# Square roots on ScalarE, an earlier warm-up and block transposes in a planned attention-plus-SwiGLU kernel

## The chip, the cores and the metric

The kernel runs on one core of a Trainium2 chip. A core has TensorE (PE, matrix multiplication into PSUM), VectorE (DVE), ScalarE (ACT), GpSimd (POOL) and SyncE (SP, which here only starts DMAs). Each takes its instructions in a fixed order from a queue of its own and waits on semaphores for the others. The metric is the device time of one execution in microseconds (us). The profile shows one execution; its span is the time from the first to the last instruction that it records.

## What is computed

All arrays are bfloat16, with 2048 rows of 512 values, 32 heads of 16 values, and a gated layer 1792 wide.

```python
xn  = layernorm(A_x)                          # no scale, no shift, eps 1e-5
q, k, v = split(xn @ wqkv)                    # 32 heads of 16
p   = softmax(q @ k.T / 4)                    # per head, 2048 x 2048
att = (p @ v).reshape(2048, 512) @ wo
ffn = (silu(xn @ w1) * (xn @ w3)) @ w2
out = A_x + att + ffn
```

## The kernel before

The heads are taken in 8 groups of four, and the queries in 4 chunks of 512. One chunk of one group is cut into *units* of 256 queries (128, 128, 256 in the first; 128 each in the last four); there are 73 units, numbered from 0. Each unit goes through these stages:

- **Pass 1** (line 1059 and line 1099). Two matmuls, one for each of two heads, write scores of 128 queries by 512 keys into two PSUM banks, and one DVE reduction takes the maximum of these 1024 columns. There are two such pairs of banks, so the next pair's matmuls run while DVE reduces. Three *splits* (lines 1088, 1168) save DVE a reduction each: ScalarE writes the Relu of a difference of two score blocks twice, and one custom DVE operation of 1024 columns takes the place of two reductions.
- **The maximum into the queries.** When a unit's reductions are done, its negated maximum (line 1235 on DVE, or six small POOL operations) becomes two more rows of the query matrix. For the first two and last four units this goes by a matmul and a copy into QT (line 821 on ScalarE; line 817 on DVE for the last unit); for the others by three DMAs.
- **Pass 2** (lines 1321, 1334, 1364). Scores again, keys by queries, with the maximum already subtracted, and ScalarE's exponential from PSUM into the buffer PT, 512 columns at a time or two banks in one instruction.
- **PV** (line 572). The exponentials against V, with a column of ones that yields the softmax denominator as row 16 of each head's 32 rows. Normally ScalarE copies the result out, and three DMAs and two POOL operations (lines 1445 to 1469) invert the denominators and multiply. For the last three units ("fast", `NFPV = 3`) DVE does it: a shuffle that copies row 16 over its head's rows, a reciprocal of 128 by 128, a multiplication (lines 1409 to 1412).
- **Column work** on TensorE between these: K, Q and V projections, the gated layer (`G`, `U`), the output (`OUT`; `OUTA` and `OUTB` for the last chunk).

**The head** is what happens before pass 1 can flow. The input lies in 16 tiles of 128 rows. For each pair of tiles the mean and variance come from DVE (lines 605, 608; tiles 0 to 7) or from two ScalarE passes (lines 595, 599; tiles 8 to 15). POOL then computes the reciprocal root by a power (lines 619, 622), and DVE (tiles 0 to 5, line 635) or POOL (tiles 6 to 15, after lines 626 and 628; line 645) normalizes. TensorE transposes a tile (line 670), and ScalarE copies it into `xnT` (line 677). Four tiles give one 512-key block of K for the first group: matmuls of line 568 and the ScalarE copy of line 701, which this text calls `KT0` to `KT3`. Pass 1 of units 0 to 2 (32 reductions) begins with the 8 that need `KT0` alone, goes on with 8 on `KT1`, and so on. While TensorE has no data it multiplies a tile of ones (line 1675); that is the warming.

**What sets the order.** A planner in the same file builds the kernel: it holds a model of each engine (when it is free, how long an operation takes, when its result is seen) and picks, over and over, the operation that can start first. `pick_pe` chooses between pass 1, pass 2, column work and filling; `pick_act`, `pick_dve`, `pick_pool` and `pick_sp` do the same for their engines. The resulting lists are what the engines run, in that order. The constants at the head of `_build` are thresholds of this planner: `_COLD` is the time up to which it counts a matmul as twice as long, `TOL` how far a piece of column work may run past the time at which a score matmul is due, `FFN_LO` and `FFN_HI` between which reductions the gated layer is spread, `SPLIT_STEP` every how many units a split stands, `PV_LEFT` how many exponentials may be missing when PV starts.

Of the kernel before, what the change touches and what calls it, by code (L numbers as in the profile page):

```python
# [13 lines left out]
_COLD = 5.9  # L14
# [239 lines left out]
def _build(nc, A_x, A_wqkv, A_wo, B_w1, B_w3, B_w2, out):  # L254
# [7 lines left out]
    NQC = S // 512  # L262
# [17 lines left out]
    TAIL_MATE = 0.3  # L280
# [3 lines left out]
    HI_LEAD = 0.0  # L284
    LAZY_MAX = 3.0
# [5 lines left out]
    A_LEAD = 0.69  # L291
# [17 lines left out]
    NFPV = 3  # L309
    NXR = 2  # L310
    FFN_LO = -60
    FFN_HEAD = 12
    FILL_P1 = 1
    FFN_HI = 800
# [5 lines left out]
    TAIL_LOW = 0  # L320
    TAIL_HIGH = 3
# [5 lines left out]
    URG_WAIT = 0.12  # L327
    FILL_SLIP = 0.03
# [3 lines left out]
    SPLIT_STEP = 6  # L332
# [21 lines left out]
    with ctx:  # L354
# [10 lines left out]
        mhalf = sb("mhalf", [128, NT], FP32)  # L365
        mone = sb("mone", [128, 8], FP32)
# [95 lines left out]

        P.op("pool", lambda e: e.memset(ones_t[:, :], 1.0), writes=[("ones_t",)], occ=0.2)
# [15 lines left out]
        P.op("dve", lambda e: e.memset(bank(7), 0.0), writes=[("ps", 7)], occ=0.5)  # L479
        P.op("pe", lambda e: e.matmul(bank(4)[:, 0:1], maskrow, onesrow[:, 0:1], start=True, stop=True),  # L480
# [7 lines left out]
        NORM = "dddppppp"  # L488
        STATS = "ddddaaaa"
        landed = [DMA_FIRST]  # L490
# [40 lines left out]
        def pad(dst, src, g):  # L531
# [5 lines left out]
                for g in range(NG - NPADQ, NG)}  # L537
        miscq.append(_Item(lambda e: e.activation(dk, sk, ACTF.Identity), [("wk",)], [("wk0",)], 0.3,
                           cb=lambda op: done.add("wk0")))
        miscq.append(_Item(lambda e: e.activation(dq, sq, ACTF.Identity), [("wq",)], [("wq0",)], 0.3,  # L540
                           cb=lambda op: done.add("wq0")))
# [44 lines left out]
        def ln_chunk(gi):  # L586
# [6 lines left out]
            if on_act:  # L593
                for t in tl:
                    act_stats.append(_Item(lambda e, t=t: e.activation(
                        a32[:, :], x_sb[:, t, :], ACTF.Identity, scale=1.0 / D, accum_out=mv[:, t, 0:1]),
                        [("PT", t)], [("a32",), ("mv", t)], 0.57, 0.7))
                for t in tl:
                    act_stats.append(_Item(lambda e, t=t: e.activation(
                        a32[:, :], x_sb[:, t, :], ACTF.Square, scale=-1.0, bias=mv[:, t, 0:1],  # L600
                        accum_out=mv[:, t, 1:2]),
                        [("PT", t), ("mv", t)], [("a32",), ("mv", t)], 0.66, 0.8, cb=lambda op: mv_done(op)))
            else:
                for t in tl:
                    dveq.append(_Item(lambda e, t=t: e.bn_stats(stats[:, t, :], x_sb[:, t, :]),
                                      [("PT", t)], [("st", t)], 0.6, 0.7, cb=lambda op, t=t: done.add(("st", t))))
                for t in tl:
                    dveq.append(_Item(lambda e, t=t: e.bn_aggr(mv[:, t, :], stats[:, t, :]), [("st", t)], [("mv", t)],
                                      0.075, 0.2, pred=lambda t=t: ("st", t) in done, cb=lambda op: mv_done(op),
                                      name="hi" if t == t1 - 1 else ""))  # L610
# [5 lines left out]

            def coef(op):
                q = poolq["ln"]
                q.append(_Item(lambda e: e.tensor_scalar(lnt[:, sl_], mv[:, sl_, 1], 1.0 / D if on_act else 1.0, EPS,
                                                         ALU.mult, ALU.add),  # L620
                               MVK, [("lnt", gi)], 0.25, 0.35))
                q.append(_Item(lambda e: e.tensor_tensor(lnr[:, sl_], lnt[:, sl_], mhalf[:, sl_], ALU.pow),
                               [("lnt", gi), ("mhalf",)], [("lnr", gi)], 0.4 + 0.16 * (t1 - t0),
                               0.5 + 0.16 * (t1 - t0), cb=norm if NORM[gi] == "d" else None))
                if NORM[gi] != "d":
                    q.append(_Item(lambda e: e.tensor_tensor(lnt[:, sl_], mv[:, sl_, 0], lnr[:, sl_], ALU.mult),
                                   [("lnr", gi)] + MVK, [("lnt", gi)], 0.25, 0.35))
                    q.append(_Item(lambda e: e.tensor_scalar(lnb[:, sl_], lnt[:, sl_], -1.0, 0.0, ALU.mult, ALU.add),
                                   [("lnt", gi)], [("lnb", gi)], 0.25, 0.35, cb=norm))

            def norm(op):
                for t in tl:
# [6 lines left out]
                    elif NORM[gi] == "a":  # L639
                        miscq.append(_Item(lambda e, t=t, xs=xs: e.activation(  # L640
                            xn_sb[:, xs, :], x_sb[:, t, :], ACTF.Identity, scale=lnr[:, t:t + 1], bias=lnb[:, t:t + 1]),
                            [("PT", t), ("lnr", gi), ("lnb", gi)], [("osb", xs)], 0.71, 0.85,
                            cb=lambda op, t=t: tr_ready(t), pred=lambda t=t: t < 4 or ("tr", t - 4) in done))
                    else:
                        poolq["nx"].append(_Item(lambda e, t=t, xs=xs: e.tensor_scalar(
                            xn_sb[:, xs, :], x_sb[:, t, :], lnr[:, t:t + 1], lnb[:, t:t + 1], ALU.mult, ALU.add),
                            [("PT", t), ("lnr", gi), ("lnb", gi)], [("osb", xs)], 0.7, 0.8,
# [142 lines left out]
        def tile_QT(q0, nq, name):  # L790
            def evac(bk):
                def cb(op):
# [3 lines left out]
                    else:  # L796
                        miscq.extend(act_stats[PRE_STATS:])
                return [_Item(lambda e: e.activation(QT[:, 0, q0:q0 + nq], bank(bk)[:, 0:nq], ACTF.Identity),
                              [("ps", bk)], qh_keys(0, q0, nq), _c_act(nq), cb=cb)]
# [573 lines left out]
        def tile_PV(u):  # L1373
# [26 lines left out]
            def evac(bk):  # L1400
                if fast:
# [7 lines left out]
                    return [_Item(lambda e: e.stream_shuffle(rp, bank(bk)[:, 0:nq], [16] * 32), [("ps", bk)],  # L1409
                                  RK, 0.21, 0.33),  # L1410
                            _Item(lambda e: e.reciprocal(rp, rp), RK, RK, 0.985, 1.13),
# [131 lines left out]
        def assign():  # L1543
# [26 lines left out]
            if p1_left[0] > 1 and p1_n[0] > 0 and not head_tiles:  # L1570
                for bk in (6, 5, 4):
                    if bk not in bank_tenant and p2_n[0] == 0:
                        if crit and ok(crit[0]):
                            give(crit.pop(0), bk)
# [6 lines left out]
        def rank(t):  # L1581
            return 0 if t.name.startswith("AQ") else 1.5 if t.name.startswith("V") else 2 if t.name.startswith("OUTB") else 1
# [84 lines left out]
        def warm_cand():  # L1667
            for bk in (5, 4):
# [3 lines left out]
                st = P.pe_start("col", None, P.ready("pe", [("ones_t",)], writes))  # L1672

# [39 lines left out]
        def pick_pe():  # L1713
# [3 lines left out]
            f = fill_cand() if ("QT", 0) in done else warm_cand()  # L1717
            def fits(x, limit):
# [66 lines left out]
        def pick_act():  # L1785
# [13 lines left out]
            for k, it in enumerate(miscq[:14]):  # L1799
                if okp(it):  # L1800
                    s = cand("act", it)
                    r = {"first": 0, "second": 1}.get(it.name, 2)
                    if m is None or s < m[0] - 1e-6 or (s < m[0] + 1e-6 and r < m[2]):
                        m = (s, k, r)
# [28 lines left out]
        def pick_dve():  # L1833
            b = None
            for q, depth in ((dveq, 8), (redq, 1)):
                for k, it in enumerate(q[:depth]):
                    if okp(it):
                        s = cand("dve", it)
                        if it.name == "hi":
                            s = max(s - HI_LEAD, 0.0)  # L1840
                        if b is None or s < b[0] - 1e-6:
                            b = (s, q, k)
            return None if b is None else (b[0], lambda: emit_item("dve", b[1], b[2]))

        def pick_pool():
            b = None
            for k in ("z", "ln", "nx", "split", "nrm", "ffn", "pad"):
                q = poolq[k]
                if q and okp(q[0]):
                    s = cand("pool", q[0])  # L1850
                    if b is None or s < b[0] - 1e-6:
                        b = (s, q)
            return None if b is None else (b[0], lambda: emit_item("pool", b[1], 0))
# [10 lines left out]
        for gi in range(len(LN_GROUPS)):  # L1864
            ln_chunk(gi)
        miscq.extend(act_stats[:PRE_STATS])
# [87 lines left out]
```

## Time and profile before

| what | value |
|---|---|
| median of 3 runs (lowest to highest) | 1194.18 us (1193.86 to 1194.46) |
| the profiled execution, own time | 1194.38 us |
| its span | 1192.6 us |
| busy: PE, DVE, ACT, POOL | 96%, 98%, 98%, 38% |
| granted TensorE clock | 0.998 of full speed |
| first and last pass-1 reduction start or end | 13.65 us, 1170.6 us |
| first and last exponential | 46.0 us, 1186.8 us |

A row of a timeline gives the start in us, the duration in us, the engine, the line, the operation, output and input, and how many were merged; a bracket tells how long the engine was idle before and for whom. Durations overlap a little, because an engine begins an instruction before the last one has been written out: the distance between two starts (the *pitch*) is what an instruction costs its queue. A row of the groups gives the busy time, the mean duration in ns, and the idle time before.

### The profile page before, as it was taken

The page shows a single profiled execution, that of the slowest core. Times are in us where ns is not written, and L with a number is a line of the kernel's source. Part 1 is how long each engine was busy: PE and PEld are TensorE (multiplying, and loading weights), DVE is VectorE, ACT ScalarE, POOL GpSimd, SP SyncE. Part 2 cuts the span into 40 slices and gives each one's busy share as a digit, 9 for nine tenths or more (in the row PEclk, how much of TensorE's full clock was granted, in tenths as well). Part 3 has the DMA queues.
Part 4 walks back from the last instruction along what each step waited for, and adds up shares of the span by engine and source line. Part 5 has one row for each costly group of instructions (what it writes and reads, how often), then busy time and mean ns, then how long its engine had stood idle before and what let it go on. Part 6 is the DMA issues. An engine that isn't in the chain of part 4 may idle for free.

```text
span 1192.6 us, 33530 instructions
## 1 busy us (share of the span) xinstructions
PE 1149.6 (96%) x13972; PEld 477.7 (40%) x13972; DVE 1173.6 (98%) x1076; ACT 1168.0 (98%) x2227; POOL 456.8 (38%) x912
## 2 busy tenths in 40 slices
PE   9999999999999999999999999999999999999997
PEld 5443333333334333333333434343333333345554
DVE  8999999999999999999999999999999999999995
ACT  7899999999999999999999999999999999999998
POOL 4453743433432246344422236734222125343320
PEclk9999999999999999999999999999999999999999
DMA  6523322111111021111100122211000111001000
GB/s 183 127 60 80 71 65 79 39 33 42 36 25 38 24 68 45 37 37 29 35 20 24 36 54 50 47 41 37 23 20 16 36 28 44 22 19 21 18 18 24
DMA packets 131188, 52.16 MB, mean 44 GB/s; under 512 B 100068, under 2 KB 131036, under 8 KB 131036
## 3 DMA queue, kind: packets, MB, share of 16 engines
q1 hardware_dynamic: 131036, 50.01, 16.8%
q8 instruction: 110, 1.80, 0.6%
q14 instruction: 42, 0.34, 0.1%
HBM read 38.73 MB, written 6.74 MB: 38 GB/s over the span
## 4 chain that ended last, share of the span: by engine, by line
ACT 43%; PE 41%; DVE 13%; issue 2%; DMA 1%; POOL 0%; ACTq 0%; POOLq 0%
ACT PT L1334 29%; PE ps L568 15%; DVE part L1099 13%; PE ps L1321 12%; ACT PT L1364 7%; PE ps L572 7%; PE ps L1059 6%; ACT zg L867 1%; ACT th L861 1%; ACT ub L871 1%; ACT U L1424 1%; ACT kq L756 1%; PE ps L1675 1%; ACT xnT L677 0%; ACT Vaug L771 0%
## 5 line engine op out<-in xcount | busy, mean ns | idle before, releaser
L1099 DVE TENSOR_REDUCE part<-ps 128x2 f32<-128x1024 f32 x1018 | 1153.0, 1212 | 1.9 <-PE ps L1059 1.7
L1334 ACT ACTIVATE PT<-ps 128x512 bf16<-128x512 f32 x1668 | 882.7, 626 | 4.5 <-PE ps L1321 1.5
L1321 PE MATMUL ps<-QT,KT 32*128 32x256 bf16 (+1 forms) x4672 | 543.4, 259 | 4.5 <-ACT PT L1364 3.7
L1059 PE MATMUL ps<-KT,QT 32*128 32x512 bf16 x2042 | 423.7, 383 | 2.4 <-DVE part L1099 2.3
L1321 PEld LDWEIGHTS ps<-QT,KT 32*128 32x128 bf16 x4672 | 206.4, 92 | 213.8 <-issue 110.9
L1449 POOL TENSOR_TENSOR Rc<-Lc,mone 128x8 f32<-128x8 f32 (+1 forms) x70 | 106.0, 1515 | 293.7 <-DMA Lc<-U 293.6
L1364 ACT ACTIVATE PT<-ps 128x1024 bf16<-128x1024 f32 x190 | 200.5, 1071 | 0.1
L568 PE MATMUL ps<-xnT,ident 128*128 128x512 bf16 (+3 forms) x642 | 176.3, 341 | 17.8 <-DVE part L1099 6.7
L572 PE MATMUL ps<-PT,Vaug 128*17 128x256 bf16 (+1 forms) x4672 | 177.3, 261 | 5.3 <-ACT PT L1364 2.2
L568 PE MATMUL ps<-xnT,w 128*128 128x512 bf16 (+3 forms) x637 | 153.1, 321 | 4.6 <-ACT ub L871 1.3
L1059 PEld LDWEIGHTS ps<-KT,QT 32*128 32x128 bf16 x2042 | 107.2, 91 | 122.9 <-DVE part L1099 57.8
L572 PEld LDWEIGHTS ps<-PT,Vaug 128*17 128x17 bf16 x4672 | 82.2, 89 | 91.5 <-issue 69.7
L568 PEld LDWEIGHTS ps<-xnT,ident 128*128 128x128 bf16 x642 | 47.0, 97 | 100.0 <-ACT PT L1334 44.6
L568 PEld LDWEIGHTS ps<-xnT,w 128*128 128x128 bf16 x637 | 44.9, 97 | 85.7 <-issue 53.0
L568 PE MATMUL ps<-w,hT 128*128 128x512 bf16 (+3 forms) x330 | 75.0, 315 | 0.0
L848 POOL TENSOR_TENSOR a<-zg,ub 128x512 f32<-128x512 bf16 x56 | 64.6, 1154 | 21.4 <-ACT ub L871 21.3
L850 POOL TENSOR_TENSOR hT<-a,t 128x512 bf16<-128x512 f32 x56 | 71.0, 1268 | 2.4
L1206 POOL TENSOR_TENSOR mx<-part 128x16 f32<-128x16 f32 (+1 forms) x67 | 14.2, 211 | 138.3 <-DVE part L1099 137.8
L1469 POOL TENSOR_TENSOR wk_on<-U,R 128x256 bf16<-128x256 f32 (+1 forms) x37 | 23.4, 632 | 88.3 <-DMA R<-rd 88.2
L1469 POOL TENSOR_TENSOR on_b<-U,R 128x256 bf16<-128x256 f32 (+1 forms) x33 | 23.4, 710 | 73.6 <-DMA R<-rd 73.6
L846 POOL TENSOR_SCALAR t<-th 128x512 f32<-128x512 bf16 x56 | 34.8, 622 | 43.0 <-ACT th L861 41.2
L861 ACT ACTIVATE th<-zg 128x512 bf16<-128x512 bf16 x56 | 37.6, 671 | 0.0
(106 smaller groups left out, 563.7 us busy)
## 6 DMA issues: line engine op xcount, KB each, us to landing
w<-in_B_w_dram SPq DMA_DIRECT2D x112, 128.0 KB
R<-rd SPq DMA_DIRECT2D x55, 128.0 KB
QT<-qd SPq DMA_DIRECT2D x31, 128.0 KB
KT<-kd SPq DMA_DIRECT2D x28, 128.0 KB
PT<-in_A_x_dram SPq DMA_DIRECT2D x4, 512.0 KB
xr<-in_A_x_dram SPq DMA_DIRECT2D x16, 128.0 KB
out_dram<-osb SPq DMA_DIRECT2D x16, 128.0 KB
qd<-kq SPq DMA_DIRECT2D x15, 128.0 KB
```

The costliest lines, as they stand in the source:

```text
L568: return e.matmul(bank(bk)[:, c0 + a:c0 + b], make_lhsT(0, 128), rhs_ap(0)[:, a:b], start=start, stop=stop, **kw)
L572: ins = e.matmul(bank(bk)[32 * i:32 * i + m, c0 + a:c0 + b], make_lhsT(i), rhs if (a, b) == (0, ncols) else rhs[:, a:b], start=start, stop ...
L848: q.append(_Item(lambda e: e.tensor_tensor(a32[:, :], zg[:, ss, :], ub[:, ss, :], ALU.mult), [("zg", ss), ("ub", ss)], [("a32",)], 1.1, 1.25))
L850: q.append(_Item(lambda e: e.tensor_tensor(hT[:, hslot(idx), :], a32[:, :], t1[:, :], ALU.mult), [("a32",), ("t1",)], [("hT", hslot(idx))] ...
L861: lazyq.append(_Item(lambda e: e.activation(th[:, ss, :], zg[:, ss, :], ACTF.Tanh), [("zg", ss)], [("th", ss)], 0.52, cb=part_done))
L1059: ins = e.matmul(bank(2 * sl + i), QT[32 * j:32 * j + 32, qs, q * 128:(q + 1) * 128], KT[32 * j:32 * j + 32, g, c_ * 512:(c_ + 1) * 512], ...
L1099: redq.append(_Item(lambda e: e.tensor_reduce(dst, pair_ap.rearrange("p (a b) -> p a b", b=512), AX.X, ALU.max), writes, [("part", par, qt ...
L1321: ins = e.matmul(bank(b)[:, i * nq:(i + 1) * nq], KT[32 * j:32 * j + 32, g, (k0 + i) * 128:(k0 + i + 1) * 128], QT[32 * j:32 * j + 32, qs, ...
L1334: expq.append(_Item(lambda e: e.activation(PT[:, sl, :], bank(b), ACTF.Exp, scale=SCALE), [("ps", b)], [("PT", sl)], _c_act(512), cb=cb, e ...
L1364: return _Item(lambda e: e.activation(PT[:, s0:s1 + 1:s1 - s0, :], ps8[:, b0:b1 + 1:b1 - b0, :], ACTF.Exp, scale=SCALE), [("ps", b0), ("ps ...
L1449: poolq["nrm"].append(_Item(lambda e: e.tensor_tensor(Rc[:, pp, 0:nl], Lc[:, pp, 0:nl], mone[:, 0:nl], ALU.pow), [("Lc", pp), ("mone",)], ...
L1469: poolq["nrm"].append(_Item(lambda e: e.tensor_tensor(onorm[ob][:, g, q0:q0 + nq], U[:, us, 0:nq], R[:, pp, 0:nq], ALU.mult), [("U", us)] ...
```

## The change

In the head, tiles 0 to 7 get their reciprocal root from a ScalarE square root and a DVE reciprocal instead of POOL's power; tiles 4 and 5 are normalized on POOL rather than on DVE; the two copies that pad the first K and Q weights move from ScalarE to POOL. ScalarE therefore loads the table for the square root first, and the one for the exponential by a dummy activation placed behind `KT3`. Five warming matmuls stand ahead of everything else on TensorE; there are 32 in all instead of 46.

The fast units become four, and the shuffle and large reciprocal are replaced by a transpose of 32 by 32 blocks, a reciprocal of 128 by 4, and a transpose back.

The planner's constants change, and several picking rules for the head (lags and ranks in `pick_act`, `pick_dve`, `pick_pool`, `rank`). In the order that results there are two splits instead of three (1020 reductions and 2 custom operations on DVE instead of 1018 and 3; 4 Relus on ScalarE instead of 6), 2048 exponentials as before in 1668 single and 190 double instructions, and 13,914 matmuls instead of 13,974.

```diff
-_COLD = 5.9
+_COLD = 8.0
...
-    TOL = 0.002
-    PV_LEFT = 5
+    TOL = 0.01
+    PV_LEFT = 6
-    PAIR_WAIT = 0.02
+    PAIR_WAIT = 0.03
-    LAZY_GAP = 0.02
+    LAZY_GAP = 0.05
-    TAIL_MATE = 0.3
+    TAIL_MATE = 0.15
+    LOW_LAG = 0.35
+    RS_LEAD = 0.4
+    HEAD_LAG = 0.7
+    HEAD_TEN = 2
+    EARLY_FILL = 5
+    FIRST_WARM = 7.75
-    A_LEAD = 0.69
+    A_LEAD = 0.7
-    NFPV = 3
+    NFPV = 4
-    FFN_LO = -60
+    FFN_LO = -20
-    FFN_HI = 800
+    FFN_HI = 700
-    TAIL_LOW = 0
-    TAIL_HIGH = 3
+    TAIL_LOW = 1
+    TAIL_HIGH = 6
-    URG_WAIT = 0.12
-    FILL_SLIP = 0.03
+    URG_WAIT = 0.16
+    FILL_SLIP = 0.02
-    SPLIT_STEP = 6
+    SPLIT_STEP = 12
...
+        P.op("dve", lambda e: e.memset(eps_t[:, :], EPS), writes=[("eps",)], occ=0.1)
+        P.op("act", lambda e: e.activation(eps_t[:, 1:2], eps_t[:, 0:1], ACTF.Sqrt), reads=[("eps",)], writes=[("eps1",)],
+             occ=0.1)
...
+        for _ in range(EARLY_FILL):
+            P.pe(lambda e: e.matmul(bank(5)[:, 0:256], ones_t[:, :], ones_t[:, :].unsqueeze(1).broadcast_to([128, 2, 128]),
+                                    start=True, stop=True),
+                 [("ones_t",)], [("ps", 5)], "col", None, _c_mm(256), name="fill")
...
-        NORM = "dddppppp"
+        NORM = "ddpppppp"
         STATS = "ddddaaaa"
+        RSTD = "aaaapppp"
...
-        miscq.append(_Item(lambda e: e.activation(dk, sk, ACTF.Identity), [("wk",)], [("wk0",)], 0.3,
+        poolq["ln"].append(_Item(lambda e: e.tensor_scalar(dk, sk, 1.0, 0.0, ALU.mult, ALU.add), [("wk",)], [("wk0",)], 0.4,
...
+            def rstd(op):
+                last = NORM[gi] == "d"
+                it = [_Item(lambda e: e.reciprocal(lnr[:, sl_], lnt[:, sl_]), [("lnt", gi)], [("lnr", gi)], 0.08, 0.2,
+                            cb=norm if last else lambda op: done.add(("rc", gi)))]
+                if not last:
+                    it.append(_Item(lambda e: e.scalar_tensor_tensor(lnb[:, sl_], mv[:, sl_, 0], -1.0, lnr[:, sl_],
+                                                                     ALU.mult, ALU.mult),
+                                    MVK + [("lnr", gi)], [("lnb", gi)], 0.08, 0.2, cb=norm, pred=lambda: ("rc", gi) in done))
+                dveq[0:0] = it
+
             def coef(op):
+                if RSTD[gi] == "a":
+                    miscq.append(_Item(lambda e: e.activation(lnt[:, sl_], mv[:, sl_, 1], ACTF.Sqrt,
+                                                              scale=1.0 / D if on_act else 1.0, bias=eps_t[:, 0:1]),
+                                       MVK + [("eps",)], [("lnt", gi)], 0.2, 0.3, name="rs" if gi < 2 else "rs2",
+                                       cb=rstd))
+                    return
...
-                    return [_Item(lambda e: e.stream_shuffle(rp, bank(bk)[:, 0:nq], [16] * 32), [("ps", bk)],
+                    t1 = U[:, us, 0:nq]
+                    t2 = U[:, us, nq:nq + nq // 32]
+                    return [_Item(lambda e: e.transpose(t1, bank(bk)[:, 0:nq]), [("ps", bk)], UK, 0.21, 0.33),
+                            _Item(lambda e: e.reciprocal(t2, t1[:, 16:nq:32]), UK, UK, 0.08, 0.2),
+                            _Item(lambda e: e.transpose(rp, t2.unsqueeze(2).broadcast_to([128, nq // 32, 32])), UK,
                                   RK, 0.21, 0.33),
-                            _Item(lambda e: e.reciprocal(rp, rp), RK, RK, 0.985, 1.13),
...
+                if FIRST_WARM < st < _COLD + 0.2:
+                    continue
...
+            if ("KT", 0, 0) not in done and P.free["pe"] > _COLD + 2.0:
+                f = None
...
+        act_stats.append(_Item(lambda e: e.activation(eps_t[:, 1:2], eps_t[:, 0:1], ACTF.Exp), [("eps",)], [("eps1",)], 1.4,
+                               pred=lambda: ("KT", 0, NQC - 1) in done))
```

More of the change, by code (lines that the diff above doesn't have):

```diff
@@ L601, in ln_chunk @@
                         accum_out=mv[:, t, 1:2]),
[L602 removed]
+                        [("PT", t), ("mv", t)], [("a32",), ("mv", t)], 0.66, 0.8, cb=lambda op: mv_done(op),
+                        name="late" if gi > 1 else ""))
             else:
@@ L1571, in assign @@
                 for bk in (6, 5, 4):
-                    if bk not in bank_tenant and p2_n[0] == 0:
+                    if (bk not in bank_tenant and p2_n[0] == 0
+                            and sum(b_ in bank_tenant for b_ in (6, 5, 4)) < (HEAD_TEN if ("KT", 0, HEAD_KT) not in done else 3)):
                         if crit and ok(crit[0]):
```

60 lines of the change are left out of this document (32 added, 28 removed).

## The prediction

> **What bounds the kernel now.** I read the page first, then the groups of instructions by form, then the waits, and last the timelines of the head and the tail. Of the groups, these:
>
> ```profile
> L1099 DVE TENSOR_REDUCE part<-ps 128x2 f32<-128x1024 f32 x1018 | 1153.0, 1212 | 1.9 <-PE ps L1059 1.7
> L1088 DVE CUSTOM_DVE_ANT_0 RB<-ps,RB 128x1024 f32<-128x1024 f32 x3 | 3.6, 1215 | 0.0
> L1334 ACT ACTIVATE PT<-ps 128x512 bf16<-128x512 f32 x1668 | 882.7, 626 | 4.5 <-PE ps L1321 1.5
> ```
>
> DVE's 1018 reductions were held up for 1.9 us in all, and 1.44 of that is before the first. So from its first reduction to its last DVE is never without work, and its queue is the clock of the kernel. ScalarE looks as full, but its mean exponential occupies 882.7 / 1668 = 0.529 us, and a dense run of them (below) has a pitch near 0.5: it has small slack between instructions. The time is therefore three pieces: until reductions flow, the reductions, and the tail after them. The head, by timelines of single engines and of all:
>
> ```profile
> 6.80 0.66 DVE L605 BATCH_NORM_STATS2 stats<-PT 128x6 f32<-128x512 bf16 x1
> 6.97 0.19 POOL L619 TENSOR_SCALAR lnt<-mv 128x2 f32<-128x2 f32 x1 [4.74 <-DVE mv L608]
> 7.25 0.71 POOL L622 TENSOR_TENSOR lnr<-lnt,mhalf 128x2 f32<-128x2 f32 x1
> 7.38 0.16 DVE L608 BATCH_NORM_AGGREGATE mv<-stats 128x2 f32<-128x6 f32 x1
> 7.46 0.66 DVE L605 BATCH_NORM_STATS2 stats<-PT 128x6 f32<-128x512 bf16 x1
> 8.12 0.70 DVE L635 TENSOR_SCALAR osb<-PT,mv,lnr 128x512 bf16<-128x512 bf16 x2
> 8.64 0.75 POOL L622 TENSOR_TENSOR lnr<-lnt,mhalf 128x2 f32<-128x2 f32 x1
> 9.41 1.08 ACT L677 ACTIVATE xnT<-ps 128x512 bf16<-128x512 bf16 x2 [1.12 <-PE ps L670]
> 9.42 0.73 DVE L635 TENSOR_SCALAR osb<-PT,mv,lnr 128x512 bf16<-128x512 bf16 x2
> 10.39 0.42 ACT L540 ACTIVATE wk_on<-wq 128x256 bf16<-128x256 bf16 x1
> 10.72 1.09 ACT L677 ACTIVATE xnT<-ps 128x512 bf16<-128x512 bf16 x2
> 11.71 0.62 ACT L595 ACTIVATE a<-PT 128x512 f32<-128x512 bf16 x1
> 12.32 0.27 ACT L798 ACTIVATE QT<-ps 128x128 bf16<-128x128 f32 x1
> 12.48 0.69 ACT L701 ACTIVATE KT<-ps,kbias 128x512 bf16<-128x512 f32 x1
> 13.65 14.79 DVE L1099 TENSOR_REDUCE part<-ps 128x2 f32<-128x1024 f32 x13 [1.44 <-PE ps L1059]
> ...
> 19.24 0.59 ACT L756 ACTIVATE kq<-ps 128x512 bf16<-128x512 f32 x1
> 19.72 0.72 ACT L599 ACTIVATE a<-PT,mv 128x512 f32<-128x512 bf16 x1
> 21.29 0.67 ACT L701 ACTIVATE KT<-ps,kbias 128x512 bf16<-128x512 f32 x1
> ...
> 41.21 2.36 DVE L1099 TENSOR_REDUCE part<-ps 128x2 f32<-128x1024 f32 x2 [0.25 <-PE ps L1059]
> 43.60 0.17 DVE L1235 TENSOR_REDUCE negm<-part 128x4 f32<-128x16 f32 x1
> ```
>
> The reader is to see POOL's power (0.71) between statistics and normalization, ScalarE's two pairs of transposed tiles with the padding of Q between them, and that reductions begin 1.17 us after the copy of `KT0` starts (12.48 to 13.65). Then 24 run at 1.137 us pitch, and the 25th, the first on `KT3`, waits 0.25. The tail:
>
> ```profile
> 1153.41 9.19 DVE L1099 TENSOR_REDUCE part<-ps 128x2 f32<-128x1024 f32 x8
> 1162.51 0.16 DVE L1235 TENSOR_REDUCE negm<-part 128x4 f32<-128x16 f32 x1
> 1162.58 8.00 DVE L1099 TENSOR_REDUCE part<-ps 128x2 f32<-128x1024 f32 x7
> 1164.06 0.28 ACT L821 ACTIVATE QT<-ps 128x128 bf16<-128x128 f32 x1
> 1164.24 6.07 ACT L1334 ACTIVATE PT<-ps 128x512 bf16<-128x512 f32 x12
> 1170.29 1.02 ACT L1364 ACTIVATE PT<-ps 128x1024 bf16<-128x1024 f32 x1
> 1171.21 1.08 ACT L1334 ACTIVATE PT<-ps 128x512 bf16<-128x512 f32 x2
> ...
> 1186.08 0.68 ACT L1334 ACTIVATE PT<-ps 128x512 bf16<-128x512 f32 x1
> 1187.28 0.30 DVE L1409 STREAM_SHUFFLE R<-ps 128x128 f32<-128x128 f32 x1
> 1187.62 0.95 DVE L1411 RECIPROCAL R<-R 128x128 f32<-128x128 f32 x1
> 1188.60 0.29 DVE L1412 TENSOR_TENSOR wk_on<-ps,R 128x128 bf16<-128x128 f32 x1
> ```
>
> Unit 71's maximum at 1162.51 releases its QT copy at 1164.06, and behind that copy ScalarE works densely for 22.5 us until 1186.76. Then PV, three DVE operations, the last output matmul and its store. So the end is tied to 1162.51, that is to DVE's queue, plus a tail that ScalarE sets.
>
> **The first reduction.** Before, POOL's two steps (6.97 to 7.96) hold up the root, and DVE passes the time with the statistics of tile 4 (7.46); normalization starts at 8.12. In the new DVE order the statistics of tile 3 (6.80 to 7.38) are followed by the reciprocal, two aggregates and the first two normalizations, and tile 4 comes after four of these. With 0.08 for each small operation (7.38 to 7.46) normalization starts at 7.62, if ScalarE's square root is done by 7.4. A square root is not in this trace; the nearest rows are ScalarE's copies, from 0.16 (12.32 to 12.48) to 0.49 (a tile copy, two in 1.08 with the overlap), and from 6.97 either ends in time or 0.1 late. The second group follows at once instead of at 9.42, so at 0.33 each the four tiles are normalized by 9.1 instead of 10.15. ScalarE's first tile copy came 1.29 after the start of normalization (8.12 to 9.41), though TensorE was busy with warming until then; I take 0.98, so 8.6. Without Q's padding (0.33 between 10.39 and 10.72) four copies at 0.49 end at 10.6; before they ended at 11.81. From there to `KT0`'s copy it was 0.67, part of it spent behind a statistics pass that began at 11.71 and has moved; I take 0.5. So `KT0` is copied at 11.1 instead of 12.48, and the first reduction comes at 11.1 + 1.17 = 12.27, a lead of 1.38. The padding now lies on POOL, which waited 4.74 for its first row above. Ends for `KT0`: 10.9, since four copies allow nothing less, and 12.1, if transposes or POOL's padding of Q come as late as they did on ScalarE.
>
> **What takes most of it back.** Eight reductions need only `KT0`; the ninth needs `KT1`, whose copy stands in ScalarE's queue. Before, 8.81 us lay between the two copies (12.48 to 21.29). In the new order two more statistics passes (0.61 each, 11.71 to 12.32) and two square roots (0.17 each) stand between them, and one spill copy of K fewer (0.48, 19.24 to 19.72): 8.81 + 1.22 + 0.34 − 0.48 = 9.89. `KT1`'s copy starts at 11.1 + 9.89 = 20.99, and the ninth reduction at 22.16. DVE would be ready at 12.27 + 8 × 1.137 + 0.16 for two small operations = 21.53, so it waits about 0.6. In the order of before the ninth came at 13.65 + 9.10 = 22.75: the lead is 0.59. The 0.25 at the 25th goes too, since `KT3`'s matmuls stand before the 23rd reduction: 0.84 in all. Ends: 1.38 + 0.25 = 1.63 less 0.16 where nothing waits, that is 1.47; and −0.15 where `KT0` comes only at 12.1. The later padding of tiles 4 and 5 on POOL (two passes more there, two fewer on DVE) is hidden by ScalarE's queue, which reaches their copies later; without that cover the ninth reduction would come later by what POOL is late.
>
> **One reduction more.** Two reductions replace one custom operation: 2 × 1.131 (9.05 / 8, from 1153.41 and 1162.51 less a 0.08 maximum) − 1.21 = +1.05 us on DVE. Two Relus fewer on ScalarE are not counted: they lie beside DVE.
>
> **The tail.** Behind unit 71's QT copy the new order has 45 exponentials, 24 of them in pairs, and one output copy; before 46, 18 in pairs. A pair has a pitch of 0.92 (1170.29 to 1171.21), a single about 0.49: 12 × 0.92 + 21 × 0.49 + 0.48 = 21.8 against 9 × 0.92 + 28 × 0.49 = 22.0. I take −0.2; ends −0.7 (the 0.5 us that ScalarE lost in this stretch gone too) and +0.5 (as much lost again, since a pair waits for two banks).
>
> **The last normalization.** Before, 1187.28 to 1188.60: 1.32 us. Transposes are not in this trace. Nearest is the shuffle of the same 128 by 128 from PSUM, pitch 0.34; the small reciprocal is nearest the maximum of 16 columns, 0.17 long, some 0.2 with its wait. 0.34 + 0.20 + 0.34 = 0.88, so −0.44. Ends: three small operations of 0.2, −0.72; two as slow as the large reciprocal, 0.98 + 0.20 + 0.98, +0.84. The fourth fast unit drops a chain of three DMAs and two POOL operations that was over 12 us before the end, and its four DVE operations fall where DVE waits for TensorE: nothing.
>
> **The other moves, at nothing.** The second table load (ScalarE, once) stands behind `KT3`; ScalarE has gaps there, and DVE does not depend on it. If that cover were gone it would cost the exponentials its length, and DVE nothing before the first lack of free banks. On SP, Q's spill now goes ahead of K's, and the fourth K spill comes from a later ScalarE copy; were it late, the 45th reduction, the first to read its block, would wait once. The planner's other thresholds reorder column work, but pass 1 against pass 2 on TensorE is the same nearly to the instruction: at the 500th pair of pass 1, 1906 pass-2 matmuls have gone before and 1904 after; at the 900th 3542 and 3546.
>
> **Sum.** 1194.38 − 0.84 + 1.05 − 0.20 − 0.44 = 1193.95. The profiled run stood 0.20 above the median, so 1193.7.
>
> [...] The warming rows, of the timeline and of two stretches of this line alone, show when the clock opens:
>
> ```profile
> 2.40 6.75 PE L1675 MATMUL ps<-ones_t 128*128 128x256 bf16 x39
> 6.90:7.40 0.50, 0.50 (x5) 1.00 1.08 344
> 7.40:7.90 0.50, 0.50 (x8) 1.00 1.10 352
> ```
>
> There are 5, then 8 matmuls per half microsecond: TensorE speeds up some 4.8 us after warming began at 2.40. [...] Only 29 warming matmuls now stand ahead of the first transpose; begun at about 1.0 they may be through before 7, and TensorE would idle until 8. [...]
>
> **Rivals.** *ScalarE is the bound, and gains.* The first exponential comes some 2.1 us sooner, since unit 0 is complete after 25 reductions instead of 26: 22.16 + 17 × 1.137 = 41.5 against 43.60. Three more copies (0.48 each) follow it, two Relus are gone: −2.1 + 1.44 − 0.96 = −1.6; with the whole lead of DVE −2.25. With tail and normalization 1191.3 to 1191.9, say 1191.5. For it: ScalarE's share is 98%. Against: 0.529 is not its pitch, and unit 71's QT copy cannot precede DVE's maximum. It decides from −2.4 on.
>
> *Reductions begin to wait.* `TOL` lets column work run 8 ns further past a score matmul's due time. If each of 1020 reductions pays that, 8.2 us; from about a third of them on (2.4 + 0.5 = 2.9 us) the kernel is slower than the bound. Half: 1193.7 + 4.1 = 1197.8. For it: DVE has no slack anywhere to absorb it. Against: reductions waited 1.9 us in all, and scores are aimed to be ready a good quarter microsecond early.
>
> **Chances.** DVE's queue as summed: 0.55. The clock closes: 0.06. ScalarE the bound: 0.20. Reductions wait: 0.19. What a measurement can tell from no change is 0.2%, 2.4 us. The first two lie within it: same 0.61, faster 0.20, slower 0.19. The likeliest case alone spans 1192.3 (lead 1.47, tail −0.7, transposes −0.72 in part) to 1195.6 (no lead, transposes slow in part). The range reaches into the rivals: 1191.3 to 1197.0.
>
> **What would show it.** First reduction near 12.3; the ninth waiting near 22.2 behind `KT1`'s copy; 1020 reductions at 1.131; unit 71's QT copy 1.55 after its maximum; about 22 us of ScalarE behind it; about 0.9 from first transpose to the multiplication. I am wrong if reductions wait for TensorE in the middle, if the ninth does not wait, or if a transpose of 128 columns takes much more than 0.34.

## The result, and the profile after

The changed kernel took 1197.81 us, median of 8 runs (1193.25 to 1199.00), against 1194.46 (1193.86 to 1194.86) of the kernel before beside it: a ratio of 1.0027, 95% interval 1.0018 to 1.0036. The profiled execution took 1197.22 us with a span of 1195.5; the granted clock was 0.995 (0.998 before). Seven of the eight runs had a clock of 0.993 to 0.996; the one of 1193.25 us had 0.999, and that split is part of the explanation below.

First the timeline of DVE in the changed kernel (start, duration, engine, line, operation; the bracket is the idle time before and its releaser):

```profile
12.25 1.23 DVE L1132 TENSOR_REDUCE part<-ps 128x2 f32<-128x1024 f32 x1
...
22.20 19.33 DVE L1132 TENSOR_REDUCE part<-ps 128x2 f32<-128x1024 f32 x17 [0.63 <-PE ps L1092]
41.56 0.17 DVE L1268 TENSOR_REDUCE negm<-part 128x4 f32<-128x16 f32 x1
...
44.12 19.32 DVE L1132 TENSOR_REDUCE part<-ps 128x2 f32<-128x1024 f32 x17
64.58 1.23 DVE L1132 TENSOR_REDUCE part<-ps 128x2 f32<-128x1024 f32 x1 [1.15 <-PE ps L1092]
66.06 1.23 DVE L1132 TENSOR_REDUCE part<-ps 128x2 f32<-128x1024 f32 x1 [0.25 <-PE ps L1354]
67.60 1.23 DVE L1132 TENSOR_REDUCE part<-ps 128x2 f32<-128x1024 f32 x1 [0.31 <-PE ps L1092]
69.62 1.23 DVE L1132 TENSOR_REDUCE part<-ps 128x2 f32<-128x1024 f32 x1 [0.79 <-PE ps L1354]
71.49 13.82 DVE L1132 TENSOR_REDUCE part<-ps 128x2 f32<-128x1024 f32 x12 [0.64 <-PE ps L1354]
...
1166.03 0.22 DVE L1268 TENSOR_REDUCE negm<-part 128x4 f32<-128x16 f32 x1
...
1190.62 0.32 DVE L1445 STREAM_TRANSPOSE U<-ps 128x128 f32<-128x128 f32 x1 [5.08 <-PE ps L590]
...
1191.54 0.29 DVE L1449 TENSOR_TENSOR wk_on<-ps,R 128x128 bf16<-128x128 f32 x1
```

The head and the last normalization came out as forecast: reductions begin at 12.25, the ninth waits 0.63 and starts at 22.20, unit 0's maximum is out at 41.56, two transposes and a small reciprocal take 0.92. What was not forecast lies between 64 and 72 us: five reductions wait 1.15 + 0.25 + 0.31 + 0.79 + 0.64 = 3.14 us. Unit 71's maximum stands at 1166.03, 3.52 later than before. The kernel before has no wait there; its reductions stand in one row of DVE's timeline without a bracket:

```profile
46.15 39.67 DVE L1099 TENSOR_REDUCE part<-ps 128x2 f32<-128x1024 f32 x35
```

What the first of the five waits for, from the timeline of PE in the changed kernel:

```profile
62.43 0.23 PE L590 MATMUL ps<-PT,Vaug 128*17 128x128 bf16 x4
64.16 0.39 PE L1092 MATMUL ps<-KT,QT 32*128 32x512 bf16 x2 [1.49 <-DMA KT<-kd]
```

The scores of the 45th reduction need a block of K, the fourth block of the second four heads. It goes by way of the buffer `kd`: one DMA writes it out (the *spill*, `kd<-kq`), two bring it into place (the *fetches*, `KT<-kd`). TensorE stands empty for 1.49 us until it lands. The same engine in stretches of 2 us (length, busy time and count, granted clock, DMA share, GB/s):

```profile
62.00:64.00 2.00, 0.66 (x16) 1.00 0.37 119
64.00:66.00 2.00, 1.84 (x32) 0.73 0.00 0
66.00:68.00 2.00, 2.00 (x53) 0.50 0.11 18
68.00:70.00 2.00, 2.00 (x32) 0.50 0.59 122
70.00:72.00 2.00, 1.83 (x17) 0.57 0.01 2
72.00:74.00 2.00, 2.00 (x18) 1.00 0.15 34
```

Behind the gap the clock falls to half. In finer stretches of the same trace it is 1.00 from 62 to 64.8 us, 0.50 from 65.0 to 71.6 and 1.00 from 71.8 to 76. With these two values alone, a stretch of 2 us at clock c has 2 × (1 − c) / 0.5 us at half speed, together 4 × (0.27 + 0.50 + 0.50 + 0.43) = 6.8 us, in which TensorE is busy nearly all the time and still too slow for DVE. These are the waits at 66 to 72.

Why the block is late, from SP's timeline of the changed kernel, and from that of the kernel before:

```profile
52.52 1.30 SPq L1262 DMA_TRANSPOSE Zs<-Z  x1
56.81 1.18 SPq L1258 DMA_DIRECT2D QT<-Zs  x2
58.09 0.61 SPq L759 DMA_DIRECT2D kd<-kq  x1
60.76 0.82 SPq L776 DMA_DIRECT2D KT<-kd  x2
```

```profile
53.40 1.30 SPq L1229 DMA_TRANSPOSE Zs<-Z  x1
54.88 0.60 SPq L727 DMA_DIRECT2D kd<-kq  x1
58.35 0.36 SPq L744 DMA_DIRECT2D KT<-kd  x1
58.77 1.16 SPq L1225 DMA_DIRECT2D QT<-Zs  x2
```

Before, the spill `kd<-kq` went right behind the DMA transpose. Now it stands behind the two transfers `QT<-Zs`, which wait for that transpose's result until 56.81 (2.9 us of waiting on SP), and it goes at 58.09 instead of 54.88. The order on SP is only a part of these 3.21 us. The spill reads what ScalarE copies into `kq`, and that copy, too, comes 2.5 us later than before. From ScalarE's timelines of the changed kernel and of the kernel before:

```profile
56.00 0.60 ACT L788 ACTIVATE kq<-ps 128x512 bf16<-128x512 f32 x1
```

```profile
53.51 0.62 ACT L756 ACTIVATE kq<-ps 128x512 bf16<-128x512 f32 x1
```

So the spill could not have gone before 56.6. About 1.7 us are the later copy and 1.5 the place in the queue; the experiment with the spill first bears this out, where it goes at 56.56, as soon as its copy is done.

### The profile page after: what moved, and what is told of

It reads as the page before. It is cut to its first block, busy times and chain, and to the rows that moved or that the text cites. A ratio compares the mean times of both kernels' runs of the same rounds, so it can differ in the third digit from the quotient of the medians.

```text
span 1195.5 us, 33264 instructions
## 1 busy us (share of the span) xinstructions
PE 1123.3 (94%) x13760; PEld 470.4 (39%) x13912; DVE 1174.3 (98%) x1083; ACT 1170.6 (98%) x2231; POOL 452.8 (38%) x901
## 4 chain that ended last, share of the span: by engine, by line
ACT 39%; DVE 36%; PE 21%; issue 2%; POOL 1%; DMA 1%; another core or an unknown queue 0%; ACTq 0%; POOLq 0%
DVE part L1132 35%; ACT PT L1367 28%; PE ps L586 7%; ACT PT L1397 7%; PE ps L1354 6%; PE ps L590 5%; PE ps L1092 3%; ACT U L1461 1%; ACT zg L900 1%; ACT th L894 1%; ACT ub L904 0%; ACT xnT L709 0%; DMA PT<-in_A_x_dram 0%; ACT kq L788 0%; POOL a L881 0%
## 5 line engine op out<-in xcount | busy, mean ns | idle before, releaser
L1354 PE MATMUL ps<-QT,KT 32*128 32x256 bf16 (+1 forms) x4672 | 536.4, 259 | 10.1 <-ACT PT L1397 5.7
L1397 ACT ACTIVATE PT<-ps 128x1024 bf16<-128x1024 f32 x190 | 198.1, 1072 | 0.2 <-PE ps L1354 0.2
L590 PE MATMUL ps<-PT,Vaug 128*17 128x256 bf16 (+1 forms) x4672 | 182.7, 262 | 4.7 <-ACT PT L1397 2.3
L586 PE MATMUL ps<-xnT,ident 128*128 128x512 bf16 (+3 forms) x580 | 161.4, 337 | 26.1 <-DVE part L1132 6.3
L586 PE MATMUL ps<-xnT,w 128*128 128x512 bf16 (+3 forms) x557 | 141.0, 327 | 8.2 <-ACT U L1461 2.9
L586 PE MATMUL ps<-w,hT 128*128 128x512 bf16 (+3 forms) x301 | 70.7, 317 | 3.4 <-ACT U L1461 2.4
```

The source lines that it names most:

```text
L586: return e.matmul(bank(bk)[:, c0 + a:c0 + b], make_lhsT(0, 128), rhs_ap(0)[:, a:b], start=start, stop=stop, **kw)
L590: ins = e.matmul(bank(bk)[32 * i:32 * i + m, c0 + a:c0 + b], make_lhsT(i), rhs if (a, b) == (0, ncols) else rhs[:, a:b], start=start, stop ...
L1354: ins = e.matmul(bank(b)[:, i * nq:(i + 1) * nq], KT[32 * j:32 * j + 32, g, (k0 + i) * 128:(k0 + i + 1) * 128], QT[32 * j:32 * j + 32, qs, ...
L1397: return _Item(lambda e: e.activation(PT[:, s0:s1 + 1:s1 - s0, :], ps8[:, b0:b1 + 1:b1 - b0, :], ACTF.Exp, scale=SCALE), [("ps", b0), ("ps ...
```

## The experiments

**The changed kernel once more**, to see how steady the picture is.

> The changed kernel as it is. Late block: most runs at 1197 to 1199 us with a granted clock of 0.993 to 0.996, now and then one near 1193.3 with 0.999; a profile of a long run has the 45th reduction waiting about 1.1 us for the block of K that SP fetches last, and one stretch of some 6.8 us at half clock right behind it. Rival, reductions waiting all over: the same times, but the reductions' idle time spread over the span and not tied to the clock.

It took 1197.85 us (1196.74 to 1198.85, 8 runs) against 1194.27 of the kernel before, ratio 1.0029 (1.0019 to 1.0039). The places are the same, the sizes vary: TensorE stands empty for 1.35 us (first row, of its timeline), DVE waits 1.23 at the 45th reduction and 0.52, 0.32, 0.79, 0.64, 0.61 and 0.18 behind it, and by stretches the clock gives 6 × 0.18 / 0.5 + 6 + 8 × 0.13 / 0.5 = 10.2 us at half speed:

```profile
63.90 0.61 PE L1092 MATMUL ps<-KT,QT 32*128 32x512 bf16 x2 [1.35 <-DMA KT<-kd]
```

```profile
60.00:66.00 6.00, 4.65 (x105) 0.82 0.19 53
66.00:72.00 6.00, 5.86 (x96) 0.50 0.24 47
72.00:80.00 8.00, 7.87 (x55) 0.87 0.23 50
```

This run, the spill first, the six matmuls and the kernel before with the late spill were measured together, beside the same 30 runs of the kernel before (1194.27 us). The other four stand beside 28 other runs of it (1194.04 us).

**The spill first.** In the finished order of SP, the one spill is moved ahead of the two transfers into QT; nothing else changes. (Of this edit and the next ones the excerpts leave out the lines that give the operations names.)

```diff
+        sp_ = P.ops["sp"]
+        at_ = [i for i, o in enumerate(sp_) if o.name == "spill_K1_3"][0]
+        sp_.insert(at_ - 2, sp_.pop(at_))
```

> The changed kernel, with one DMA start moved on SP's queue: the fourth K spill goes ahead of the two DMAs that carry unit 2's maximum into QT. Late block: the spill starts 1.5 us sooner, at 56.6, its block lands at 62.6 instead of 64.1, the 45th reduction no longer waits (minus 1.15) and the clock stays open (minus 2.0): 1193.3 to 1194.1 us in every run, clock 0.998 or 0.999. Reductions waiting all over: no change, above 1196.5. Clock closing for lack of TensorE work whatever the DMA does: minus 1.15 alone, about 1196.

1193.27 us (1193.04 to 1193.64, 11 runs), ratio to before 0.9993 (0.9984 to 1.0001). SP's timeline, and DVE's group of all reductions (busy us, mean ns, idle us before):

```profile
56.56 0.60 SPq L759 DMA_DIRECT2D kd<-kq  x1
57.26 1.14 SPq L1259 DMA_DIRECT2D QT<-Zs  x2
59.23 0.81 SPq L777 DMA_DIRECT2D KT<-kd  x2
```

```profile
L1133 DVE TENSOR_REDUCE part<-ps 128x2 f32<-128x1024 f32 x1020 | 1155.0, 1207 | 0.6 <-PE ps L1093 0.6
```

One spill 1.5 us sooner (56.56 instead of 58.09, and its fetches as much) takes 4.58 us off the kernel (1197.85 to 1193.27). 1020 reductions now wait 0.6 us in all, and that is the ninth's wait. So the rival by which reductions wait all over, because `TOL` is wider, is out: `TOL` is as wide here.

**Late, but TensorE kept busy.** The changed kernel with the spill where it was, and six matmuls of 512 columns, whose result nothing reads, put into the queue between the wait for the PSUM banks and the wait for the block.

```diff
+                if isinstance(k, tuple) and e == "pe" and getattr(op, "pre", None) is not None:
+                    op.pre(handle)
+                    op.pre = None
...
+        keep = [o for o in P.ops["pe"] if o.name == "p1_44"][0]
+        def keep_warm(e):
+            for _ in range(6):
+                e.matmul(bank(0), ident[:, :], xnT[:, 0, 0:512], start=True, stop=True)
+        keep.pre = keep_warm
```

> The changed kernel, with six matmuls of 512 columns put in front of the 45th pair of pass 1, behind its wait for DVE and ahead of its wait for the block of K, so that TensorE works 1.3 of the 1.5 us that it idled. Late block with the clock as its second half: the 45th reduction still waits about 1.1 us, the clock stays open, 1195.0 to 1196.0 us. If the wait itself did the whole harm: 1197 to 1199 as before. If the added matmuls get in the way: above 1199.

1194.6 us (1194.25 to 1195.08, 11 runs), ratio 1.0004 (0.9995 to 1.0013). DVE's timeline has the wait of the 45th reduction and none behind it:

```profile
64.72 20.52 DVE L1135 TENSOR_REDUCE part<-ps 128x2 f32<-128x1024 f32 x18 [1.29 <-PE ps L1095]
```

By stretches the clock is 1.00 from 60 to 80; the one in which the changed kernel had 0.50:

```profile
66.00:72.00 6.00, 5.95 (x115) 1.00 0.23 47
```

This splits the loss of 4.58: the late block by itself costs 1194.6 − 1193.27 = 1.3 us, as much as its one wait; the clock that closes on an empty TensorE costs the other 1197.85 − 1194.6 = 3.25.

**Half the filling.** Three matmuls instead of six, beside the other set of runs of the kernel before (1194.04 us, 28 runs).

> The changed kernel with three instead of six filling matmuls of 512 columns ahead of the 45th reduction's scores, on TensorE, while the fourth K block is still on its way. It asks how long TensorE may stand before the clock closes: about 1.5 us stood empty as changed, about 0.2 us with six, and about 0.85 us should stand empty with three. If a stand of 0.85 us is harmless: clock 1.00 from 60 to 80 us, the 45th reduction still waits 1.2 to 1.3 us, 1194.6 us as with six. If any stand of this kind closes the clock: the granted clock is near 0.5 for two or three stretches of 3.4 us, and the time is 1197 to 1198. If it depends on where the stand falls: runs in two groups, near 1194.6 and near 1197.5.

1194.61 us (1194.36 to 1196.53, 11 runs), ratio 1.0004 (0.9995 to 1.0013). TensorE now stands empty for 0.69 us before the block (timeline of PE), and the clock stays at 1.00:

```profile
62.55 0.82 PE L1941 MATMUL ps<-xnT,ident 128*128 128x512 bf16 x3
64.07 0.39 PE L1095 MATMUL ps<-KT,QT 32*128 32x512 bf16 x2 [0.69 <-DMA KT<-kd]
```

Ten of the eleven runs lie at 1194.36 to 1194.88 with a clock of 0.997 to 0.999, one at 1196.53 with 0.996. In the 16 runs of the changed kernel as it is, 15 had 0.993 to 0.996. So at this place the kernel with a gap of 0.69 us in its profile kept the clock in nearly all its runs, and the changed kernel (1.49 and 1.35 us in its two profiles) in nearly none. The expectation's stretches of 3.4 us are an estimate from the 6.8 and 10.2 us at half speed in those two profiles, as two and three of equal length; none was seen alone.

It is not the length alone. TensorE stands empty in other places as well, and there the clock stayed at 1.00: for 1.10 us before 13.32 in the first profile of the changed kernel, for 1.32 us before 1179.43 in the kernel before, and in the head for 1.97 us with the spill first. Of the last, a row of PE's timeline and a stretch:

```profile
7.97 0.40 PE L702 MATMUL ps<-ident,osb 128*128 128x128 bf16 x4 [1.97 <-DVE osb L672]
```

```profile
6.00:8.00 2.00, 0.03 (x1) 1.00 1.09 348
```

In the head the granted clock alone says little: in the kernel before it reads 1.00 both at 6.90 to 7.40, where 5 warming matmuls run, and at 7.40 to 7.90, where 8 do. So the durations have to be read beside it. TensorE had sped up ahead of that gap: the 24 warming matmuls before it take 3.60 us (from 2.40 to 6.00, where the gap begins), where they take 4.96 in the changed kernel's profile. And it stayed fast: the four matmuls behind the gap take 0.40, and 0.39 in the kernel before, where no gap stands ahead of them. What else decides is not shown.

**The kernel before with the late spill.** The same mistake made in the other kernel: spill and fetches moved behind the transfers into QT.

```diff
+        sp_.insert(at_, sp_.pop(at_ + 2))
+        sp_.insert(at_ + 1, sp_.pop(at_ + 3))
```

> The kernel before, with the same DMA start moved the other way: its fourth K spill goes behind the two DMAs of unit 2's maximum. Late block: the spill starts at about 58.9 instead of 54.9, the 45th reduction waits 1 to 2 us, and where the clock closes behind it another 2 to 3 us: 1196.0 to 1199.0 us, in two groups of runs. Rival, that only the new order as a whole is sensitive: 1195 to 1196, clock 0.998.

A miss: 1194.2 us (1193.84 to 1195.35, 11 runs), ratio 1.0001 (0.9992 to 1.0010). Its timelines of SP, of PE and of DVE:

```profile
59.31 0.61 SPq L727 DMA_DIRECT2D kd<-kq  x1
61.97 0.83 SPq L745 DMA_DIRECT2D KT<-kd  x2
```

```profile
64.07 0.39 PE L1060 MATMUL ps<-KT,QT 32*128 32x512 bf16 x2 [0.33 <-DMA KT<-kd]
```

```profile
46.23 40.98 DVE L1100 TENSOR_REDUCE part<-ps 128x2 f32<-128x1024 f32 x36
```

The scores came at 64.07, hardly sooner than in the changed kernel (64.16), yet no reduction waited. (The spill goes 1.2 us later here, but from the first fetch to the scores it is 2.1 us, 61.97 to 64.07, where it was 3.4 in the changed kernel, 60.76 to 64.16; why is open.) The difference is when the scores are due. Here 28 reductions are done at 46.23, so the 45th is due 16 pitches later, at 46.23 + 16 × 1.137 = 64.4; in the changed kernel 27 are done at 44.12, and it is due at 44.12 + 17 × 1.137 = 63.4. The lead of the head had brought the need forward by 1.0 us, while the block came no earlier.

**The kernel before with a later spill still**, behind two weight loads and a small store as well.

```diff
...
+        for k_ in (2, 3, 4):
+            sp_.insert(at_ + k_, sp_.pop(at_ + k_ + 3))
```

> The kernel before with the fourth K spill and the two transfers that fetch the block moved behind the two transfers into QT and also behind two weight loads and one small store on SP, some 1.5 us further than in the run before, which was absorbed. The scores of the first reduction on that block would then wait on TensorE for about 1.8 us instead of 0.33, of which DVE's queue covers something between 0.3 and 1. Theory (a late block makes DVE wait, and an empty TensorE closes the clock, in whichever kernel): the granted clock falls near 0.5 for two or three stretches of 3.4 us around 66 to 76, DVE waits 0.5 to 1.3 us at the block and some tenths behind it, 1196.5 to 1198.5 us. Rival (the clock is a matter of the changed kernel's other column order alone): clock 1.00, the wait alone, 1194.8 to 1195.5. Rival (the kernel before has slack for this too): no wait on DVE, 1194.2.

1198.25 us (1197.33 to 1198.56, 6 runs), ratio 1.0032 (1.0020 to 1.0043): the kernel before now has the changed kernel's fault, and about its time. Its timelines of PE and of DVE, then PE by stretches:

```profile
66.23 0.61 PE L1060 MATMUL ps<-KT,QT 32*128 32x512 bf16 x2 [2.80 <-DMA KT<-kd]
```

```profile
66.88 3.76 DVE L1100 TENSOR_REDUCE part<-ps 128x2 f32<-128x1024 f32 x3 [2.78 <-PE ps L1322]
71.47 13.87 DVE L1100 TENSOR_REDUCE part<-ps 128x2 f32<-128x1024 f32 x12 [0.83 <-PE ps L1322]
```

```profile
64.00:66.00 2.00, 0.00 (x0) 0.69 0.41 119
66.00:68.00 2.00, 1.77 (x35) 0.50 0.11 22
68.00:70.00 2.00, 2.00 (x32) 0.50 0.12 33
70.00:72.00 2.00, 2.00 (x14) 0.60 0.03 2
```

The gap is 2.80 us, the clock falls to half for 6.8 us here too, and no line of the head, no threshold and no column order of the changed kernel is in it. The time is the expected one, its parts are not: the block makes DVE wait 2.78 us, where 0.5 to 1.3 was expected, and behind it only 0.83 more. In the changed kernel the larger part lies behind the block. So this run shows that a late block does the harm in this order as well, and that the clock falls with it, but it does not repeat the split of 1.3 and 3.25.

**Spill first, and one reduction fewer.** The changed kernel with the spill moved as above and `SPLIT_STEP` set back, to have three custom operations and 1018 reductions.

```diff
-    SPLIT_STEP = 12
+    SPLIT_STEP = 6
```

> The changed kernel with the fourth K spill ahead of the transfers into QT, and with the step of the units that use the custom operation set back to 6, so that there are three custom operations and 1018 reductions again. By the sum of the prediction, one reduction more costs 1.05 us on DVE: 1193.27 - 1.05 = 1192.2 us, unit 71's maximum 1.05 us earlier. If ScalarE is the bound (the rival): no gain or little, 1193.0 to 1193.3, and DVE waits for banks near the end. If the new plan disturbs the middle: reductions wait, above 1193.5.

1193.7 us (1193.33 to 1194.92, 11 runs), ratio 0.9996 (0.9987 to 1.0005): 0.34 below its runs of the kernel before, where the spill alone was 1.00 below its own; no gain. DVE's timeline of this run:

```profile
330.86 392.64 DVE L1133 TENSOR_REDUCE part<-ps 128x2 f32<-128x1024 f32 x347 [0.47 <-PE ps L1093]
...
1161.88 0.16 DVE L1269 TENSOR_REDUCE negm<-part 128x4 f32<-128x16 f32 x1
```

The planner made another order of the rest with it. A reduction waits 0.47 that did not, and unit 71's maximum is 0.27 sooner than with the spill alone (1161.88 against 1162.15) instead of 1.05. Behind the maximum even that is lost: the copy of unit 71 into QT comes at 1164.03, and it came at 1163.95 with the spill alone and at 1164.06 in the kernel before, although the maxima stood at 1161.88, 1162.15 and 1162.51. From the maximum to the end of the span it is 30.0 us here (1191.9 − 1161.88) and 29.15 with the spill alone (1191.3 − 1162.15). So this run does not price the reduction. In its order of work the 0.27 did not reach the end; whether it would in another, it does not show.

**The transposes alone**, in the kernel before, in its three fast units. The excerpt is shortened to the calls.

```diff
-  stream_shuffle(rp, bank(bk)[:, 0:nq], [16] * 32)
-  reciprocal(rp, rp)                                    # 128 x 128
+  transpose(t1, bank(bk)[:, 0:nq])                      # 32 x 32 blocks
+  reciprocal(t2, t1[:, 16:nq:32])                       # 128 x 4
+  transpose(rp, t2.unsqueeze(2).broadcast_to([128, nq // 32, 32]))
```

> The kernel before with block transposes and a reciprocal of four columns in place of the shuffle and the reciprocal of 128 columns, in its last three units; nothing else is changed. By the prediction's 0.88 for three operations against 1.32, 0.44 us less at the end: 1193.8 us beside 1194.3. As the profile of the changed kernel shows it, 0.40. If the last normalization is hidden: 1194.3. If the transposes only look short because the bank is ready: 0.98 for one of them, 1194.5 to 1195.1.

1193.82 us (1193.17 to 1194.01, 11 runs), ratio 0.9995 (0.9986 to 1.0004). DVE's timeline:

```profile
1186.74 0.32 DVE L1412 STREAM_TRANSPOSE U<-ps 128x128 f32<-128x128 f32 x1 [4.43 <-PE ps L572]
...
1187.65 0.29 DVE L1416 TENSOR_TENSOR wk_on<-ps,R 128x128 bf16<-128x128 f32 x1
```

0.91 instead of 1.32: the step is 0.41 shorter. The medians differ by 0.22 with an interval that holds 0 and 0.41, so the time does not decide between them. In the profiles the end shows it: from unit 71's maximum to the end of the span it is 29.65 us here (1191.6 − 1161.95) and 30.09 in the kernel before (1192.6 − 1162.51), 0.44 less; in the two runs with the late spill, which end by the old operations, it is 30.0 and 30.1. Transposes that take 0.98 each are out.

## Why the prediction was wrong

It said 1193.7 with a range up to 1197.0; the measurement is 1197.81. By its own steps:

- **The first reduction**: forecast 12.27, found 12.25. A square root takes 0.30 us, and `KT0` is copied at 11.06 (11.1). Right.
- **What takes most of it back**: `KT1`'s copy at 21.05 (20.99), the ninth reduction at 22.20 after 0.63 of waiting (22.16, 0.6). Between the maxima of unit 0, one reduction less, the lead is 43.60 − 1.14 − 41.56 = 0.90; forecast 0.84. Right, and with some luck in the profile: in the three runs made from the kernel before, whose head is the same, that maximum stands at 43.09, 43.37 and 43.67, so one profile gives the lead only to some 0.6 us.
- **One reduction more**, +1.05: too high by some 0.4. With the spill first, the maximum of unit 71 came 0.36 before the old one, where −0.84 + 1.05 = +0.21 was forecast. From the reduction behind unit 1's maximum to unit 71's maximum it is 1118.10 us there (44.05 to 1162.15) and 1116.36 in the kernel before (46.15 to 1162.51), with one reduction more in this stretch besides: 1.74 − 1.13 = +0.61. The sum set the custom operation at its duration, 1.21, where it holds the queue for 1.13 to 1.15 (724.08 to 725.21, for one); by that it would have been +1.12. On the other side the kernel before loses 0.2 in waits too short to show in the timeline (1.9 in its group, less 1.44 and 0.25), and the kernel with the spill first none. The other 0.3, a third of a nanosecond for each reduction, was not pursued.
- **The tail and the last normalization**, −0.20 and −0.44: from unit 71's maximum to the end of the span it was 30.09 (1192.6 − 1162.51) and is 29.47 in the changed kernel (1195.5 − 1166.03): −0.62 in place of −0.64. Of it 0.40 is the normalization. In the kernels with the changed order it lies between 29.14 and 29.66, so that the agreement to 0.02 is luck; the order of the run with one reduction fewer gave it all back (30.0).
- **The step that failed** is among "the other moves, at nothing": that the fourth K spill, "were it late", would make the 45th reduction "wait once". The place was named, and so was the later ScalarE copy; the price was put at zero in the sum without asking when the spill would go and when the block would be needed. Both could be read in part. The block had 1 us less, because the head's lead moves every reduction up by 0.9 to 1.0; the copy comes 2.5 us later; and on SP the spill had come to stand behind transfers that wait for a DMA transpose. The wait is 1.15 us in the profile and costs 1.3. That alone would have given about 1195.
- **"Once" was wrong as well.** While DVE waits for a DMA, TensorE is empty, and here that closed its clock: another 3.25 us, more than twice the wait. The prediction gave a clock that closes a chance of 0.06, and the one place at which it let TensorE idle is the head, until 8. There TensorE stood empty for 0.66 us, with the clock at 1.00 and the four transposes behind it at 0.40, and nothing of a fall was seen. The stretches at half speed were 6.8 us twice and 10.2 us once. Gaps of 1.35, 1.49 and 2.80 us went with them; one of 1.97 us in the head did not.
- **ScalarE as the bound**, the rival at 1191.5, was not met; whether ScalarE decides nearer to the forecast is open. The copy of unit 71 into QT stood at 1164.0 within 0.1 in three kernels whose maxima differ by 0.63, but each of the three has an order of its own. Where the order is the same, the copy keeps its distance from the maximum: 1.49 to 1.55 in the kernel before and the three runs made from it (maxima from 1161.95 to 1166.51), 1.80 to 1.87 in the changed kernel and the three runs with its order (1162.15 to 1167.06). So the sign that the prediction gave, 1.55, came out 0.25 to 0.32 longer in the new order. **Reductions that wait** came in the measured time, 1197.8, but not by its mechanism: they wait at one place and for a DMA, and `TOL` has no part in it.

With the one spill moved, the time is near the forecast: 1193.27 beside 1194.27, that is −1.0 where −0.43 was summed up, the difference lying mostly in the reduction and the tail above. This version has the lowest median here; its interval against the kernel before still touches 1.

One thing stays open: the one run of the changed kernel at 1193.25 us with a clock of 0.999, as fast as with the spill moved. It fits a block that landed in time, since with the clock kept open and the block late no run was under 1194.25, but there is no profile of it.

## What to carry over

Whoever makes an early stage faster has to go through the transfers that feed the next stages and set for each the new time of need against the new time of issue, in queue order: a gain in the head is a loss of slack for all that is loaded later (here 1.0 us at the 45th reduction). A DMA that must wait should stand in its queue behind those that need not (here one spill moved ahead of two waiting transfers was worth 4.58 us). A wait that leaves TensorE empty is priced with the clock it may cost (here 3.25 us on top of 1.3), not by its own length; if it can't be avoided, matmuls that nobody reads can be worth their place in the queue, as here with those 3.25 us.

## What was not expected of the hardware

Gaps in the matmuls of 1.49 and 1.35 us, in an otherwise full stream, halved the granted clock for 6.8 and 10.2 us in the two profiles of the changed kernel; a gap of 2.80 us halved it for 6.8; a gap of 0.69 us left it at 1.00 in the profile, and by time and mean clock in ten of eleven runs. In other places 1.10, 1.32 and 1.97 us left it at 1.00, so the length alone does not decide. Nor is the fall tied to the end of the gap: the matmuls that ended the gap of 1.49 at 64.16 still took 0.39 us, and the clock fell between 64.8 and 65.0, while the ones that ended the gaps of 1.35 and 2.80 took 0.61, the clock having fallen before.
